# Redistributing rows and columns of one shared piece among the sixteen DMA engines in a grouped 1x1 convolution

## The chip, the cores and the metric

The kernel runs on one core of a Trainium2 chip. The metric is the device time of one execution in microseconds (us), as the median of several runs. The profile is of one execution, and its span goes from the first to the last instruction.

## The reference

The input `x` has shape (1, 512, 512, 192) in bf16 and is read as 262,144 pixels of 192 channels. The kernel size is 1, so there is no neighbourhood and no padding. The channels are split into four groups of 48, and each group is multiplied by a 48 x 48 matrix of its own:

```
H = W = 512;  G = 4;  Cg = 48;  C = 192;  k = 1
xg  = x.reshape(B, H, W, G, Cg)
out = einsum('bhwgc,gcd->bhwgd', xg, w[0, 0])      # reshaped to (B, H, W, C)
```

Every pixel is 384 B in and 384 B out, so 100.66 MB are read and as many written.

## The kernel before

**Ring and pieces.** A ring in SBUF, 128 rows by 520 pixel columns, holds pixels before and after the multiplication; results overwrite inputs in place. It has five slots of 104 columns (`BIG`). `plan_pieces` cuts all pixels into pieces. The first slot is loaded in four pieces of 8, 20, 28 and 32 columns (`HEAD`); then come full pieces of 104 columns by 128 rows; the remainder, smaller than 104 columns, is the last piece. A full piece of n columns gives each of the 128 rows n consecutive pixels, so that a row is one packet of n x 384 B, and each of the 16 DMA engines moves eight rows.

**The shared piece.** After nine full slots one piece is inserted that fills only some rows, by the tuple `SHARED`. Each entry is (first row, rows, parts, columns, queue):

```
SHARED_COLS = 72
SHARED = ((0, 16, 4, SHARED_COLS, SYNC), (32, 16, 4, SHARED_COLS, SYNC), (52, 44, 11, 64, POOL))
CURSOR = 5
```

Two blocks of 16 rows go in four parts through SP's queue (loads) and ACT's queue (stores), so that four DMA engines, called 0 to 3 here, hold eight of these rows each. A block of 44 rows goes in eleven parts through the GpSimd queue; a copy of five rows just before it moves that queue's position, so that engines 5 to 15 hold four of these rows each. Engine 4 holds none of the shared piece. The shared piece holds 32 x 72 + 44 x 64 = 5,120 pixels, and `plan_pieces` gives the other pieces what is left: (262,144 - 5,120) / 128 = 2,008 columns, of which 88 are the head, 18 x 104 the full pieces and 48 the last piece. Rows and columns of the shared piece's slot that hold no pixels are computed too, and not stored.

**Compute.** The unit is a group of four pixel columns. TensorE transposes a group in six 128 x 128 blocks into PSUM (L247), VectorE copies two groups at a time from PSUM to SBUF (L286), TensorE multiplies (L262) with block-diagonal weights that are built at the start, and ScalarE copies the result back into the ring (L304). There are 520 groups, taken in 260 pairs.

**Order.** SP issues the loads (L217) piece by piece. Before the load of a slot it waits until the store of the piece five slots back has landed on all engines (`wait_slot`). ACT issues a store (L298) when the groups of that part have been copied; pieces in the last slots but one are stored in two halves of 52 columns (`LATE_PARTS`), and the last piece, being smaller than 104 columns, in one. GpSimd issues the load and the store of its block (L199), each behind its five-row copy (L197). The DMA engines work the queues of SP, ACT and GpSimd, and instruction fetches, side by side.

Of the kernel before, what the change touches and what calls it, by code (L numbers as in the profile page):

```python
# [28 lines left out]
LATE_PARTS = (52, 52)  # L29
LAST_PARTS = (32, 32, 24, 16)  # L30
SHARED_AT = (9,)
SHARED_COLS = 72
SYNC, POOL = 0, 1
SHARED = ((0, 16, 4, SHARED_COLS, SYNC), (32, 16, 4, SHARED_COLS, SYNC), (52, 44, 11, 64, POOL))
CURSOR = 5
NXP = 4
NXS = 3
# [39 lines left out]
def plan_pieces(npix):  # L77
    few = sum(rows * cols for _, rows, _, cols, _ in SHARED)
    at = list(SHARED_AT)
    if npix < len(at) * few + 128 * (sum(HEAD) + BIG * (at[-1] + 2)):  # L80
        at = []
    cols = (npix - few * len(at)) // 128
    assert cols % 4 == 0
    head = list(HEAD) if cols >= sum(HEAD) + BIG else []
    mid = cols - sum(head)
    slots = [[(BIG, None)]] * (mid // BIG) + ([[(mid % BIG, None)]] if mid % BIG else [])
    for i in at:
        slots.insert(i, [(SHARED_COLS, SHARED)])
    if head:
        slots.insert(0, [(s, None) for s in head])  # L90
    pieces, g, pix = [], 0, 0
    for n, parts in enumerate(slots):
        c = n * BIG % RCOLS
        for s, shares in parts:
            pieces.append(Piece(len(pieces), n, c, g, s, shares, pix))
            c, g, pix = c + s, pieces[-1].g1, pieces[-1].pix_end
    assert pix == npix
    return pieces
# [240 lines left out]
```

## Time and profile before

| | us |
|---|---|
| median of 3 runs | 483.42 (482.58 to 484.23) |
| profiled execution | 483.69 |
| its span | 480.8 |
| PE busy | 430.3 |
| ACT busy | 391.9 |
| DVE busy | 249.6 |
| mean rate of all DMA | 421 GB/s |
| HBM read and written | 100.68 MB and 100.66 MB |

The profile numbers the DMA queues: q1 is SP's, q10 is ACT's, q0 is GpSimd's; q8 and q14 carry instructions. A packet in the trace is one row of one transfer on one engine, with its start, its duration and its size; the record does not name the engine. The semaphore of a transfer rises when an engine has finished its part. PE's busy share counts pipelined matmuls and says little about how near PE is to its peak.

### The profile page before, as it was taken

What the parts mean: (1) busy time and instruction counts of PE and PEld (TensorE: products, weight loads), DVE (VectorE), ACT (ScalarE), POOL (GpSimd) and SP (SyncE); (2) the same over time, 40 slices, a digit from 0 to 9 for tenths busy, and PEclk for the clock granted to TensorE, in tenths of its full rate; (3) what the DMA queues carried; (4) which work ended last, traced back from release to release, by engine and by line L of the source; (5) the groups of instructions that cost most, each with busy time, mean ns of one, the idle gap of its engine ahead of it and who ended that gap; (6) DMA issues with size and microseconds to landing.
All of it is one profiled execution on the core that took longest, in us unless ns stands there. A gap on an engine that the chain in (4) does not pass through costs nothing.

```text
span 480.8 us, 13914 instructions
## 1 busy us (share of the span) xinstructions
PE 430.3 (89%) x6250; PEld 390.5 (81%) x6250; DVE 249.6 (52%) x261; ACT 391.9 (81%) x521; POOL 3.7 (1%) x12
## 2 busy tenths in 40 slices
PE   5979999999999999999679998989898999999910
PEld 5878898898898899889578887978787898898810
DVE  2535655655655655565335553545454556556500
ACT  2959999999998999899649995979797989999920
POOL 1000000000000001000000000000000000000000
PEclk9989999999999999999979998999999999999965
DMA  8999999999999999999999999999999999999995
GB/s 329 428 436 434 413 432 415 413 421 433 428 433 427 438 421 427 423 439 430 428 423 438 434 418 438 435 423 430 431 427 435 432 428 426 420 423 431 428 422 233
DMA packets 7913, 202.22 MB, mean 421 GB/s; under 512 B 1176, under 2 KB 1176, under 8 KB 1688
## 3 DMA queue, kind: packets, MB, share of 16 engines
q1 hardware_dynamic: 3560, 99.60, 48.5%
q10 hardware_dynamic: 4072, 99.58, 48.5%
q0 software_dynamic: 224, 2.16, 1.1%
q8 instruction: 49, 0.80, 0.6%
q14 instruction: 8, 0.07, 0.0%
HBM read 100.68 MB, written 100.66 MB: 419 GB/s over the span
## 4 chain that ended last, share of the span: by engine, by line
PE 47%; another core or an unknown queue 24%; DMA 23%; SPq 1%; issue 1%; ACT 0%
PE o_ps L262 27%; PE xT_ps L247 20%; DMA ring<-in_x_dram 13%; DMA out_dram<-ring 10%; SPq L217 1%; ACT ring L304 0%; SPq L213 0%; SPq L51 0%
## 5 line engine op out<-in xcount | busy, mean ns | idle before, releaser
L304 ACT CAST ring<-o_ps 128x768 bf16<-128x768 f32 x520 | 390.6, 802 | 68.0 <-PE o_ps L262 57.4
L286 DVE COPY xT_sb<-xT_ps 128x1536 bf16<-128x1536 bf16 x260 | 249.0, 958 | 205.1 <-PE xT_ps L247 205.1
L262 PE MATMUL o_ps<-wt,xT_sb 128*128 128x144 bf16 (+1 forms) x3120 | 290.6, 235 | 5.7 <-ACT ring L304 1.8
L262 PEld LDWEIGHTS o_ps<-wt,xT_sb 128*128 128x128 bf16 x3120 | 210.8, 98 | 43.1 <-ACT ring L304 32.8
L247 PE MATMUL xT_ps<-ident,ring 128*128 128x128 bf16 x3120 | 221.6, 222 | 20.9 <-DMA ring<-in_x_dram 20.5
L247 PEld LDWEIGHTS xT_ps<-ident,ring 128*128 128x128 bf16 x3120 | 190.8, 99 | 23.1 <-DMA ring<-in_x_dram 20.1
L197 POOL DMA_DIRECT2D cur<-in_x_dram x2 | 1.2, 622 | 242.7 <-DMA out_dram<-ring 188.8
L230 PE MATMUL o_ps<-w_sb,esel 48*128 48x48 bf16 x10 | 0.6, 209 | 2.8 <-DMA w_sb<-in_w_dram 2.8
L230 PEld LDWEIGHTS o_ps<-w_sb,esel 48*128 48x128 bf16 x10 | 0.4, 111 | 2.8 <-issue 2.8
L280 DVE CAST wt<-o_ps 128x480 bf16<-128x480 f32 x1 | 0.7, 658 | 3.4 <-PE o_ps L230 3.4
L304 ACT ACT_TABLE_LOAD x1 | 1.3, 1283 | 0.8 <-PEq L324 0.8
L199 POOL DMA_DIRECT2D ring<-in_x_dram x1 | 0.6, 563 | 0.0
L199 POOL DMA_DIRECT2D out_dram<-ring x1 | 0.6, 559 | 0.0
L184 POOL TENSOR_SCALAR_AFFINE_SELECT esel<-esel 48x272 bf16<-48x272 bf16 x1 | 0.4, 402 | 0.0
L181 POOL MEMSET esel<- 48x272 bf16 x1 | 0.3, 317 | 0.3 <-POOLq L324 0.3
L188 POOL TENSOR_SCALAR_AFFINE_SELECT ident<-ident 128x128 bf16<-128x128 bf16 x1 | 0.3, 282 | 0.0
L182 POOL MEMSET ident<- 128x128 bf16 x1 | 0.2, 198 | 0.0
L324 POOL MEMSET const-bfloat16-1.0<- 128x1 bf16 x1 | 0.1, 101 | 0.0
L324 POOL MEMSET const-uint8-127<- 128x1 uint8 x1 | 0.1, 101 | 0.0
L324 POOL MEMSET const-float32-0.0<- 128x1 f32 x1 | 0.1, 98 | 0.3 <-issue 0.3
L324 POOL MEMSET const-float32-1.0<- 128x1 f32 x1 | 0.1, 98 | 0.0
## 6 DMA issues: line engine op xcount, KB each, us to landing
ring<-in_x_dram SPq DMA_DIRECT2D x18, 4992.0 KB, 33.4
out_dram<-ring ACTq DMA_DIRECT2D x13, 4992.0 KB, 51.4
out_dram<-ring ACTq DMA_DIRECT2D x10, 2496.0 KB, 43.5
ring<-in_x_dram SPq DMA_DIRECT2D x1, 2304.0 KB, 16.3
out_dram<-ring ACTq DMA_DIRECT2D x1, 2304.0 KB, 19.7
ring<-in_x_dram SPq DMA_DIRECT2D x1, 1536.0 KB, 11.1
out_dram<-ring ACTq DMA_DIRECT2D x1, 1536.0 KB, 40.8
ring<-in_x_dram SPq DMA_DIRECT2D x1, 1344.0 KB, 7.9
```

The costliest lines, as they stand in the source:

```text
L181: gp.memset(esel[:], 1.0).then_inc(p0_sem, 1)
L184: gp.affine_select(out=esel[:], in_=esel[:], pattern=[[-1, ECOLS]], compare_op=AluOpType.is_equal, fill=0.0, base=ESHIFT, channel_multipli ...
L197: gp.dma_start(cur[:, n], few).then_inc(cur_sem, 16)
L199: gp.dma_start(*((sbuf, dram) if inward else (dram, sbuf))).then_inc(done, 16)
L217: sp.dma_start(sbuf, dram).then_inc(ld_sem[p.i], 16)
L230: last = pe.matmul(o_ps[:, NOB - 1, col:col + CG], lhsT=esel[:, s0:s0 + 128], rhs=w_sb[:, g, :], start=True, stop=True, skip_group_check=True)
L247: last = pe.transpose(xT_ps[:, g % NXP, j * 128:(j + 1) * 128], xg[:, j * 128:(j + 1) * 128], ident[:])
L262: last = pe.matmul(o_ps[:, v % NOB, c0_:c1_], lhsT=xs[:, j * 128:(j + 1) * 128], rhs=wt[:, WOFF[tc]:WOFF[tc] + (c1_ - c0_)], start=(tc == ...
L280: dve.tensor_copy(wt[:], o_ps[:, NOB - 1, 0:WCOLS]).then_inc(wc_sem, 1)
L286: dve.tensor_copy(xT_sb[pair % NXS][:, 0:n * 2 * UC].rearrange("p (g c) -> p g c", g=n), xT_ps[:, b0:b0 + n, 0:2 * UC]).then_inc(e_done, 1)
L304: act.copy(dst, o_ps[:, v % NOB:v % NOB + 2, 0:UC]).then_inc(fa_done, 1)
L324: nc = _bacc.Bacc("TRN2", target_bir_lowering=False, num_devices=1)
```

## The change

The two blocks on engines 0 to 3 get 56 columns where they had 72. The block on engines 5 to 15 keeps 64, which is now the widest, so the piece's own size falls from 72 to 64 columns.

```
-SHARED_COLS = 72
+SHARED_COLS = 64
 SYNC, POOL = 0, 1
-SHARED = ((0, 16, 4, SHARED_COLS, SYNC), (32, 16, 4, SHARED_COLS, SYNC), (52, 44, 11, 64, POOL))
+SHARED = ((0, 16, 4, 56, SYNC), (32, 16, 4, 56, SYNC), (52, 44, 11, 64, POOL))
```

By the formula of `plan_pieces` the shared piece now holds 32 x 56 + 44 x 64 = 4,608 pixels, the rest is 2,012 columns, and the last piece has 52 columns instead of 48. The groups become 519: 16 instead of 18 in the shared piece, 13 instead of 12 in the last.

## The prediction

> **What bounds the kernel now.** I read the page first: its busy times, its DMA row, its queue table.
>
> ```profile
> PE 430.3 (89%) x6250; PEld 390.5 (81%) x6250; DVE 249.6 (52%) x261; ACT 391.9 (81%) x521; POOL 3.7 (1%) x12
> ...
> DMA  8999999999999999999999999999999999999995
> ...
> q1 hardware_dynamic: 3560, 99.60, 48.5%
> q10 hardware_dynamic: 4072, 99.58, 48.5%
> q0 software_dynamic: 224, 2.16, 1.1%
> q8 instruction: 49, 0.80, 0.6%
> q14 instruction: 8, 0.07, 0.0%
> ```
>
> No compute engine is over 89%, while the queues add up to 98.7% of sixteen DMA engines' span. The loads are q1, the stores q10, the pool's two copies q0; q8 and q14 fetch instructions through the same engines. The chain of waits names PE (47%), but in a kernel that is full on the DMA side this only says who was late at a buffer. So next the view by windows (columns: stretch, PE, PEld, DVE, ACT, POOL, clock, DMA share, GB/s).
>
> ```profile
> 100.00:190.00 90.00, 89.09 (x1318) 80.58 (x1316) 52.66 (x55) 82.12 (x110) 0.00 (x0) 1.00 1.00 429
> 190.00:300.00 110.00, 99.06 (x1413) 90.20 (x1411) 56.23 (x59) 88.49 (x119) 2.36 (x4) 0.95 1.00 430
> 438.00:468.00 30.00, 20.97 (x306) 18.63 (x304) 12.02 (x13) 21.00 (x28) 0.00 (x0) 0.89 1.00 428
> 468.00:481.00 13.00, 0.00 (x0) 0.00 (x0) 0.00 (x0) 0.00 (x0) 0.00 (x0) 0.50 0.55 238
> ```
>
> After the first 20 us the DMA share stands at 1.00 up to 468, whatever PE does. In the last 13 us no engine computes and the DMA engines finish at different times (share 0.55). The DMA view of the last 3.2 us, in forty slices of 80 ns, and the timeline of ACT's end show the rest:
>
> ```profile
> DMA  0900000000900000005500000000000000000000
> GB/s 0 461 0 0 0 0 0 0 0 0 461 0 0 0 0 0 0 0 230 230 0 0 0 0 0 0 0 0 0 0 0 0 0 0 0 0 0 0 0 0
> DMA packets 8, 0.11 MB, mean 35 GB/s; under 512 B 2, under 2 KB 2, under 8 KB 2
> ```
> ```profile
> 460.67 0.34 ACTq L298 DMA_DIRECT2D out_dram<-ring  x1
> ```
>
> Six large packets, in three pairs: two engines work alone for the last 2.2 us. The last store was issued at 460.67, 19 us earlier, so they are not waiting for anything; they still have a queue. The end is set by whichever DMA engine has most to do.
>
> **Which engine has most.** In the trace's packet records each packet starts 3 ns before the one ahead of it on its engine ends, so sixteen streams can be followed back from their last packets. Their ends, and what the streams hold from 185 us on:
> - three end at 468.1, 468.6, 468.7: pool packets, hardly any fetches;
> - eight end at 475.8, 475.9, 476.1, 476.5, 476.7, 476.7, 476.7, 477.7: most q8 fetches, and pool packets;
> - one ends at 476.2: its packets are longer, 1493 and 1578 ns by turns where others take 1476. It is engine 4 by its sum: without that it would have ended some 7 us ahead of the three;
> - four hold the 27,648 B packets of the blocks of 72 columns, so they are engines 0 to 3: 476.9, 477.3, 480.0, 480.0. The two last also hold the q14 fetches.
>
> Here and there a packet falls to a neighbour in this following; the ends and the 27,648 B packets are clear. The groups check by size: a row of one column costs 768 B in and out, 28.4 ns by the 39,936 B packet (1476 ns for 104 columns one way). Engines 0 to 3 carry 8 x 2008 + 576 = 16,640 of them (472 us), engines 5 to 15 carry 16,320 (463 us), engine 4 16,064 (456 us). The first packets start at 2.3 us. Forty-nine fetches on eight engines make six each and one with seven; at about 1.0 us and 0.3 us for the longer packet behind it, that is the 8 us by which the eight end after the three, and the odd one is the stream at 477.7.
>
> **The change, part by part.**
> 1. *Engines 0 to 3, shared piece.* Each moves 8 packets in and 8 out. A packet falls from 27,648 B (1025 ns) to 21,504 B; on the line between 18,432 B (686 ns) and 39,936 B (1476 ns) that is 799 ns. 16 x 226 ns = 3.62 us less on each.
> 2. *All engines, last piece.* The 512 pixels given up make the last piece 52 columns instead of 48. Each engine moves 8 packets in and 8 out at 742 instead of 686 ns (the 19,968 and 18,432 B packets): 16 x 56 ns = 0.90 us more on each.
> 3. *Compute.* The shared piece falls from 18 groups to 16, the last rises from 12 to 13: 519 groups instead of 520. Twelve matmuls, one ACT copy and half a DVE copy go. One more group now follows the last load: ACT's 802 ns step puts the last store at about 461.5. The earliest stream reaches it at 462.6 + 0.45 (its longer load) = 463.0; a packet started 1.7 us after its issue at the head (1.25 to 2.94), so the three early streams could idle 0.2 us of their 9 us. The rest reach it after 470. Costed at nothing; without that cover it would be 0.8 us.
> 4. *Waits.* SP's load of a slot waits for all sixteen engines of the store five slots back, so the laggards 0 to 3 hold it up (the store issued at 318.4 lands its first twelve parts by 331.7, the last at 346.3, and the load starts at 346.32). Their lag shrinks, so loads start no later. No stall goes away, because the share is 1.00 already. The pool's block, its two cursor copies and the queues they pass stay as they are.
>
> The sum: engines 0 to 3 end 2.72 us earlier (474.1, 474.6, 477.3, 477.3); all others 0.90 later: engine 4 at 477.1, the three at 469.6, the eight at 476.7 to 478.6. What is late next is the stream with the seventh fetch. The end moves from 480.0 to 478.6, 1.4 us earlier: half of what is taken off the old bound, since the new one was 2.3 us behind and is pushed 0.9. The profiled execution, 483.69, has span 480.8 and 2.9 around it; it would become 482.3. It stands 0.27 above the median, 483.42, so the forecast is 482.1.
>
> The size of a fetch is the term without a clean row: its packet is about 1.0 us, what it adds behind it 0.3 to 0.5. Moving one fetch from or to the last of the eight is worth 1.3 us either way, so the gain lies between 0.1 and 2.7; I take the ends as this execution has them.
>
> The Trainium skill ("Runtime: NRT & Kernel Launch", Instruction fetch mechanics) says that instructions come in 16 KiB blocks and that crossing one is mostly hidden; the trace agrees on the block (16,384 B packets), but the eight streams that have them end 8 us after the three that hardly do. By that page alone the full gain of 2.7 us would come.
>
> **Rivals.**
> *Full gain.* If the fetches fall otherwise (one block fewer, as 24 of PE's instructions go, or the odd one on an early stream), the eight end near 477.5, almost level with the pair, and the gain comes up to its own 2.7: 483.42 - 2.7 = 480.7. For it: the odd fetch is a single packet. Against: 24 of PE's 12,500 are 0.2%, a tenth of one of its 49 blocks. 12%.
>
> *One shared ceiling.* If the engines share a limit, balance is worth nothing: the same 201 MB take as long, 483.4. For it: 428 to 430 GB/s in all full stretches. Against: in the last 2.2 us, with fourteen engines silent, the two still take 686 ns for 18,432 B, as when all ran. 8%.
>
> The Trainium skill ("DMA: Bandwidth & Descriptors", Specifications) gives about 358 GB/s of HBM for one core and 27 GiB/s for an engine; by the first the transfer as a whole would bind and this change would do nothing, but the rows show 430 GB/s.
>
> *Slower: engines 0 to 3 don't bind in an ordinary run.* The pair leads by 2.3 us only through q14's eight packets (0.07 MB). Without them it would end near 477.3, the eight would set the end already at 477.7, and the change would add its 0.90: 484.3. It decides once the pair's lead over the eight falls under 0.90 us. A seventh or eighth fetch on the wrong stream (1.3) makes it 485.6. For it: fetch times differ from run to run, and the three runs spread by 1.65 us. Against: the instructions are there in every run, profiled or not, and the profiled run is near the median. 22%.
>
> **How the numbers follow.** The forecast's case gets 58%. A measurement of this kernel tells about 0.3% (1.45 us) from no change, and 1.4 us is right at that line: it splits nearly evenly, 28% faster and 30% same. Full gain adds 12% to faster; the shared ceiling adds 8% to same; the slower case gives 10% to same (its 0.9 us is 0.19%) and 12% to slower. Faster 40%, same 48%, slower 12%. The range goes from 480.6, which takes in the full gain, to 484.2, which takes in all but the far end of the slower case. The forecast's own range is 481.2 to 483.2.
>
> **What would show it.** The packets of the shared piece on q1 and q10 at about 0.80 us; the last large packets in one stream or two near 478.6 and 18 or 19.97 KB large; DMA share still 1.00 up to about 469; in the last stretch a share above 0.55; the last store issued near 461.5; 519 ACT copies. It is wrong if the engines with the small shared packets are again the last, if the share falls below 0.99 in mid-span (a load came late), or if the last streams end after 480.

## The result: 1.3 us less, and the profile after

The changed kernel takes 481.82 us (median of 10 runs, 481.15 to 483.10), the kernel before 483.22 in the same series (median of 10). The ratio is 0.9973, with a 95% interval of 0.9960 to 0.9986: about 1.3 us or 0.27% faster (1.4 us between the medians). The prediction said 482.1 and a gain of 1.4. The profiled execution took 481.49, with a span of 479.4; the span fell by 1.4 us, the rest of its difference (483.69 to 481.49) lies in what surrounds the span, 2.1 us instead of 2.9.

The page after, the same lines:

```profile
PE 429.6 (90%) x6238; PEld 390.7 (81%) x6238; DVE 249.2 (52%) x261; ACT 391.3 (82%) x520; POOL 3.7 (1%) x12
...
DMA  8999999999999999999999999999999999999996
...
q10 hardware_dynamic: 4072, 99.58, 48.6%
q1 hardware_dynamic: 3560, 99.60, 48.6%
...
q8 instruction: 49, 0.80, 0.6%
q14 instruction: 8, 0.07, 0.0%
...
L304 ACT CAST ring<-o_ps 128x768 bf16<-128x768 f32 x519 | 390.0, 802 | 69.6 <-PE o_ps L262 62.7
```

Packets and bytes of every queue are the same to the last digit; only the span over which they are spread is shorter (48.5 to 48.6% each). The windows after (stretch, PE, PEld, DVE, ACT, POOL, clock, DMA share, GB/s):

```profile
100.00:190.00 90.00, 88.99 (x1327) 81.09 (x1325) 52.73 (x56) 82.61 (x111) 0.00 (x0) 1.00 1.00 430
190.00:300.00 110.00, 99.27 (x1439) 90.27 (x1437) 57.30 (x61) 90.05 (x121) 2.37 (x4) 0.97 1.00 430
438.00:468.00 30.00, 22.03 (x320) 19.56 (x318) 12.74 (x14) 21.80 (x29) 0.00 (x0) 0.92 1.00 428
468.00:481.00 13.00, 0.00 (x0) 0.00 (x0) 0.00 (x0) 0.00 (x0) 0.00 (x0) 0.50 0.55 237
```

The stretches in the middle moved as many bytes per us as before; the gain lies in how the last queues end. Three views show that end: the DMA engines from 474.0 to 481.0 us (forty slices of 175 ns; a packet counts in the slice in which it starts, the last one in slice 22), the packet count from 477.8 us on, where before a pair of engines had six large packets left, and the last store on ACT's timeline.

```profile
DMA  7755957575775770075002000000000000000000
```
```profile
DMA packets 4, 0.00 MB, mean 0 GB/s; under 512 B 4, under 2 KB 4, under 8 KB 4
```
```profile
461.68 0.34 ACTq L298 DMA_DIRECT2D out_dram<-ring  x1
```

Nothing that starts after 477.8 is a data packet any more; the last one, begun just before, ends at 478.5. Followed back through the packet records in the same way as before, the sixteen streams end as follows. Where two packets end at the same moment, the following can swap two streams; the set of ends does not depend on that.

| streams | before | forecast | after |
|---|---|---|---|
| engines 0 to 3, without fetches | 476.9, 477.3 | 474.1, 474.6 | 474.3, 474.4 |
| engines 0 to 3, with q14 fetches | 480.0, 480.0 | 477.3, 477.3 | 477.8, 478.0 |
| eight with q8 fetches | 475.8 to 477.7 | 476.7 to 478.6 | 476.7 to 478.5 |
| engine 4 | 476.2 | 477.1 | 477.4 |
| three early | 468.1 to 468.7 | 469.6 | 468.9 to 469.2 |

The bound went from the pair with q14 to one of the eight, as forecast.

### The profile page after: what moved, and what is told of

The parts are those of the page before. It is cut to its first block, busy times and chain, and to the rows that moved or that the text cites. A ratio compares the mean times of both kernels' runs of the same rounds, so it can differ in the third digit from the quotient of the medians.

```text
span 479.4 us, 13889 instructions
## 1 busy us (share of the span) xinstructions
PE 429.6 (90%) x6238; PEld 390.7 (81%) x6238; DVE 249.2 (52%) x261; ACT 391.3 (82%) x520; POOL 3.7 (1%) x12
## 2 busy tenths in 40 slices
DMA packets 7913, 202.22 MB, mean 422 GB/s; under 512 B 1176, under 2 KB 1176, under 8 KB 1688
## 3 DMA queue, kind: packets, MB, share of 16 engines
q10 hardware_dynamic: 4072, 99.58, 48.6%
q1 hardware_dynamic: 3560, 99.60, 48.6%
## 4 chain that ended last, share of the span: by engine, by line
PE 48%; DMA 42%; another core or an unknown queue 5%; issue 1%; ACT 1%; SPq 1%
PE o_ps L262 28%; DMA ring<-in_x_dram 23%; PE xT_ps L247 20%; DMA out_dram<-ring 19%; ACT ring L304 1%; SPq L217 0%; SPq L213 0%
## 5 line engine op out<-in xcount | busy, mean ns | idle before, releaser
L247 PEld LDWEIGHTS xT_ps<-ident,ring 128*128 128x128 bf16 x3114 | 190.3, 99 | 22.2 <-DMA ring<-in_x_dram 19.4
```

The lines of the kernel that those rows point to most:

```text
L247: last = pe.transpose(xT_ps[:, g % NXP, j * 128:(j + 1) * 128], xg[:, j * 128:(j + 1) * 128], ident[:])
```

## The experiments

The theory: all sixteen engines work without a pause, so the time is set by the engine with the largest sum of packets. The rivals: one ceiling shared by all engines, so that balance is worth nothing and the gain came from elsewhere; and, for the terms of the sum, fetches that cost nothing. Ratios are to the kernel before, timed in each run's own series; "above the changed kernel" is the difference of two such ratios.

**One step back the other way.** 88 columns on engines 0 to 3.

Against the kernel before:

```
-SHARED_COLS = 72
+SHARED_COLS = 88
```

> Engines 0 to 3 hold 88 columns of the shared piece, the last piece has 44 columns: the step opposite to the change. Theory (the most loaded DMA engine sets the end): against the kernel before, engines 0 to 3 carry 3.62 us more in the shared piece and 0.90 less in the last, so the last pair of streams ends at 480.0 + 2.7 = 482.7 and the time rises by 2.7 us, ratio 1.0056. Rival (one ceiling shared by all engines; what the change gained came from elsewhere): the bytes are the same, so the ratio is 1.000.

Measured: 485.85 us, ratio 1.0058 (1.0046 to 1.0070), where 1.0056 was expected. The view of the DMA engines from 480.0 to 484.1 (forty slices of 0.1 us) has two streams left, one 0.9 us longer:

```profile
DMA  0300300300300300300300000300000000000000
GB/s 0 165 0 0 165 0 0 165 0 0 165 0 0 165 0 0 165 0 0 165 0 0 0 0 0 165 0 0 0 0 0 0 0 0 0 0 0 0 0 0
```

Their last packets end at 482.4 and 483.3; 482.7 was forecast. The same data took 2.8 us more (0.58% of 483), so a shared ceiling does not set the time.

**One step further.** 40 columns on engines 0 to 3, the last piece 56. This edit and those below are against the changed kernel.

```
-SHARED = ((0, 16, 4, 56, SYNC), (32, 16, 4, 56, SYNC), (52, 44, 11, 64, POOL))
+SHARED = ((0, 16, 4, 40, SYNC), (32, 16, 4, 40, SYNC), (52, 44, 11, 64, POOL))
```

> Engines 0 to 3 hold 40 columns, the last piece has 56: a second step in the direction of the change. Theory: the engines with instruction fetches are the bound now and get 0.90 us more, 478.5 + 0.9 = 479.4, while the streams of engines 0 to 3 end near 471.6 and 475.2. Against the kernel before the time is 0.6 us lower, ratio 0.9988, and it is 0.8 to 0.9 us above the changed kernel. Rival (the blocks on engines 0 to 3 still set the end): another 1.3 us is gained, ratio 0.9946.

Measured: 482.68 us, ratio 0.9994 (0.9985 to 1.0003): it lies 0.0021 above the changed kernel's ratio, 1.0 us, where 0.8 to 0.9 was expected. The last data packet ends at 479.8 (forecast 479.4), alone for its last 1.1 us; the view is from 476.0 to 481.0 (slices of 125 ns):

```profile
DMA  7330933730940830040000030000000000000000
```

So taking still more from engines 0 to 3 loses most of what the first step won: they no longer set the end, and the 0.90 us that everyone gets for it is paid in full. With 88, 72, 56 and 40 columns the ratios are 1.0058, 1, 0.9973 and 0.9994, a V whose two sides are the two terms of the sum.

**The first term alone.** 56 columns, but the last piece stays at 48: this kernel leaves out the last 512 pixels of the image.

```
-    pieces = plan_pieces(npix)
+    pieces = plan_pieces(npix - 512)
```

> The first part of the change alone: engines 0 to 3 hold 56 columns, the last piece keeps 48, and the 512 pixels between (the last of the image) are neither loaded nor computed nor stored. Theory: the pair of engines 0 to 3 ends 3.6 us earlier, at 476.4 to 477.0, the eight with fetches stay at 475.8 to 477.7; the end moves from 480.0 to about 477.7, so 2.3 us less than before, ratio 0.9953, and 0.9 us less than the changed kernel. Rival (shared ceiling): only the 0.2% of bytes left out is gained, 0.9 us, ratio 0.998.

Measured: 480.68 us, ratio 0.9947 (0.9935 to 0.9959), where 0.9953 was expected and the shared ceiling gave 0.998. The last data packet ends at 477.6 (forecast 477.7), the two streams of engines 0 to 3 without fetches at 473.2 and 473.6, 3.7 us earlier than before (forecast 3.6). The bytes left out are 0.39 of 202.22 MB, 0.2%, where the ratio fell by 0.53%:

```profile
DMA packets 7913, 201.83 MB, mean 422 GB/s; under 512 B 1176, under 2 KB 1176, under 8 KB 1688
```

The changed kernel's 0.9973 is 0.0026 above this, 1.3 us for the second term, 0.9 by the sum and between the ends (477.6 and 478.5); the intervals hold both.

**More fetches.** Nothing but instructions is added.

```
+                for _ in range(4):
+                    dve.wait_ge(wb_sem, 1)
```

> The changed kernel with four waits more in each of DVE's 260 steps, on a semaphore that has long been reached: no work and no data, but 1,040 instructions of 64 B, 67 kB or eight fetches of 8,192 B more on q14. Theory (a fetch costs its engine's queue 0.3 us and 0.3 to 0.4 in the packet behind it, and q14 serves one stream of engines 0 to 3 for each engine that fetches): the stream that serves DVE ends 5 to 6 us later, 478 + 5.5 = 483.5, and the time is about 5 us above the changed kernel, ratio to the kernel before 1.007. If they spread over both streams, 2 to 2.5 us above it, ratio 1.002. Rival (crossing a block is hidden, and the end is not set by these streams): the time of the changed kernel, ratio 0.997.

Half as many came out as were meant (why is open); the page counts them (13,889 instructions in the changed kernel):

```profile
span 482.1 us, 14410 instructions
...
q8 instruction: 49, 0.80, 0.6%
q14 instruction: 12, 0.10, 0.0%
```

These are 521 instructions and four fetches more on q14. In the packet records four of q14's twelve stand about where four stood in the changed kernel; the other four have become eight, some 50 to 75 us apart. Measured: 484.61 us, ratio 1.0027 (1.0016 to 1.0039), which is 2.6 us above the changed kernel. The DMA view of the last 3.4 us shows one engine alone:

```profile
DMA  0005000000005000000005000000000000000000
...
DMA packets 4, 0.06 MB, mean 18 GB/s; under 512 B 1, under 2 KB 1, under 8 KB 1
```

It ends at 481.2, the other fifteen by 478.6. The ratio alone would also fit the branch in which eight fetches spread over two streams (1.002); that one stream is late, and that four came instead of eight, is in the trace. Its place before was 477.8 or 478.0, so four fetches cost it 3.2 to 3.4 us, 0.8 us each; the expectation's 0.6 to 0.7 was a little low. So a fetch is not free for the DMA engine that carries it. That one stream took all four also shows that here DVE's fetches went through one DMA engine, on q14, while the 49 blocks on q8 went through several.

**Which engines are early.** The pool's block is split in two, of three and of eight engines; the five-row copy stands before the first alone (that edit is not shown).

```
+SHARED_COLS = 96
+SHARED = ((0, 16, 4, 54, SYNC), (32, 16, 4, 54, SYNC), (52, 12, 3, SHARED_COLS, POOL), (64, 32, 8, 54, POOL))
```

> The pool's block is split: engines 5 to 7 hold 4 rows of 96 columns, engines 8 to 15 4 rows of 54, engines 0 to 3 8 rows of 54; the last piece has 52 columns as in the changed kernel. Theory, with the guess that the three streams that end near 469 are engines 5 to 7: against the changed kernel these three get 3.6 us more (to 472.7), the eight with fetches 1.1 less (477.4), engines 0 to 3 0.45 less (477.6). The end comes near 477.6, ratio to the kernel before 0.995. If the early three are other engines, streams with fetches get the 3.6 us and the end comes near 481 to 482, ratio 1.002 to 1.004. Rival (shared ceiling, or compute: the shared piece has 24 groups, 8 more to compute): no gain over the changed kernel, ratio 0.997 to 1.00.

Measured: 485.00 us (483.49 to 485.47), ratio 1.0030 (1.0019 to 1.0041): the guess that engines 5 to 7 are the early ones was wrong, and the branch for that (1.002 to 1.004) came in. In the profiled execution, 483.80 us, two streams end at 480.9 and 481.2, when all others have ended by 478.1: two of engines 5 to 7 do fetch, one does not.

> A look at which DMA engines the early streams are. The pool's block is cut into five blocks of two engines each, with columns of their own as a mark: engines 5 and 6 hold 50 columns, 7 and 8 54, 9 and 10 58, 11 and 12 62, 13 and 14 64, engine 15 none; the last piece has 56 columns. The size of its shared packets then names a stream's pair. Theory, after the split of 3 and 8 engines: one of engines 5 to 7 and two of 8 to 15 end 7 to 8 us ahead of the others, and hold no 16,384 B fetches, and every stream's end follows its sum. The time itself is no question: by the sums it is 0.5 to 1.5 us above the changed kernel. Rival (the early streams are not tied to engines): the early three show other marks than these groups allow.

The five-row copy stands once before the five loads and, with six rows, once before the five stores. The edit of the tuple (that of the copies is not shown):

```
+SHARED = ((0, 16, 4, 56, SYNC), (32, 16, 4, 56, SYNC),
+          (52, 8, 2, 50, POOL), (60, 8, 2, 54, POOL), (68, 8, 2, 58, POOL), (76, 8, 2, 62, POOL), (84, 8, 2, 64, POOL))
```

One execution was timed: 492.49 us. By the marks, both streams of 54 columns (engines 7 and 8) are without fetches, as is one of the two streams without a mark (engine 15; the other has the longer packets and is engine 4). So engines 7, 8 and 15 are the early ones, and the split before agrees (one of 5 to 7, two of 8 to 15). The time was off by far more than the 0.5 to 1.5 us that was called no question. The reason is in the issues (KB, us from issue to landing) and in the windows:

```profile
ring<-in_x_dram POOLq DMA_DIRECT2D x1, 192.0 KB, 61.5
...
ring<-in_x_dram POOLq DMA_DIRECT2D x1, 186.0 KB, 50.9
...
ring<-in_x_dram POOLq DMA_DIRECT2D x1, 174.0 KB, 38.2
...
ring<-in_x_dram POOLq DMA_DIRECT2D x1, 162.0 KB, 25.4
...
ring<-in_x_dram POOLq DMA_DIRECT2D x1, 150.0 KB, 17.9
```
```profile
190.00:240.00 50.00, 32.75 (x481) 29.33 (x478) 19.32 (x21) 31.14 (x42) 3.39 (x6) 0.88 1.00 429
240.00:300.00 60.00, 42.92 (x619) 39.44 (x619) 24.22 (x26) 37.69 (x50) 3.28 (x6) 0.84 0.98 405
300.00:346.00 46.00, 45.89 (x677) 41.34 (x676) 27.09 (x29) 42.14 (x57) 0.00 (x0) 1.00 0.93 382
```

Five transfers of the pool's queue land one after the other, 8 to 13 us apart, though each has different engines; in the changed kernel a single one of 1,056 KB landed in 19.4 us. The shared piece was complete at 255 us, PE stood for 32 us (its longest wait for a load is 32.3 us), and the queues behind it ran dry: the share falls to 0.98 and 0.93. Compute never caught up; the last store was issued at 478.8 us, 17 us later than in the changed kernel. Here a stall cost time; in the four kernels of the V the share stayed at 1.00 up to 468 us.

**A flatter distribution.** With these marks, engines 7 and 8 were given more and the rest less; the five-row copy stands once before the three transfers (that edit is not shown).

```
-SHARED_COLS = 64
+SHARED_COLS = 104
+SHARED = ((0, 16, 4, 48, SYNC), (32, 16, 4, 48, SYNC),
+          (52, 8, 2, 48, POOL), (60, 8, 2, SHARED_COLS, POOL), (68, 28, 7, 48, POOL))
```

> A try at a flatter distribution, with the marks of the run before: engines 7, 8 and 15 fetch no instructions. Engines 7 and 8 hold 4 rows of 104 columns, engines 5, 6 and 9 to 15 4 rows of 48, engines 0 to 3 8 rows of 48, the last piece has 56 columns; the pool's block goes in three transfers of 2, 2 and 7 engines. By the sums alone, against the changed kernel: the streams with fetches 0.9 us less (477.6), the pair with q14 0.9 less (477.0), engine 4 0.9 more (478.2), engines 7 and 8 5.5 more (474.5): the end near 478, ratio to the kernel before 0.996, about 0.4 us better than the change. Rival (the three pool transfers land one after the other, as the five did in the run before): the shared piece is complete at about 230 us instead of 211, PE stands 5 to 10 us, and if the queues of stores run dry behind it the time is 1 to 5 us above the changed kernel, with a DMA share under 1.00 between 240 and 346 us.

Measured: a median of 487.61 us over twelve runs. Six took 482.3 to 485.6 us, with ratio 1.0007 (0.9991 to 1.0024), so no gain; the other six took 489.6 to 494.2, with granted clocks like the rest (0.957 to 0.974). In the profiled one, 483.59 us, the pool's three loads landed 16.9, 28.2 and 41.0 us after their issue and PE waited up to 12 us for a load, but the share stayed at 1.00, and all streams but two ended by 478.3, as the sums said; two ended at 480.5, and whose they are stays open. Whether the six long runs have the stall of the run before is open too: none of them was profiled. A version that beats the changed kernel was not found.

## Why the prediction was right

- *What bounds.* The prediction read the end as that of the fullest of sixteen engines, from the last two streams working alone for 2.2 us. The V of four column counts and the run with fetches alone show it: each moved the end by about what it put on one group of streams, with the data unchanged. In all of these runs, and with the first term alone, the stream that ends last can be followed back over more than 200 us with no gap above 3 ns between its packets.
- *Engines 0 to 3, 3.62 us less.* The packet of 21,504 B took 799 ns, as the prediction's line between two other sizes gave it. With the first term alone the streams without fetches ended 3.7 us earlier.
- *Last piece, 0.90 more.* The packet took 742 ns. The eight moved from 475.8 to 477.7 up to 476.7 to 478.5.
- *What is late next.* The forecast end of 478.6 was measured at 478.5. The pair with q14 fell only 2.0 to 2.2 us instead of 2.7, to within 0.5 of the new bound; the early three came up to 0.7 sooner than forecast and engine 4 0.3 later. The size of a step was right on the streams that set the end; single streams scatter by half a microsecond, so an agreement within 0.1 us is partly luck. So is the margin: the prediction took the spread of the fetches from one execution and put 1.3 us on one fetch more or less, and the odd block of 49 might have fallen elsewhere.
- *Compute.* The page counts 519 ACT copies. The last store was issued at 461.7 (forecast 461.5) and no stream that sets the end waited for it.
- *Waits.* Loads did start earlier. The store that the prediction reads as held up to 346.3 was complete at 336.6 after, and the load behind it began then, as the chain of work shows (start, us; the first line before, the others after):

```profile
346.32 38.06 DMA ring<-in_x_dram
```
```profile
293.27 43.33 DMA out_dram<-ring
336.62 47.92 DMA ring<-in_x_dram
```

The prediction gives the issue of that store as 318.4; that is the next store, and this one was issued at 294.9 before and 293.3 after. The reading that its last parts hold up the load stands. The 10 us bought nothing that shows: the DMA share was 1.00 around it in both kernels.
- *A sign badly chosen.* A share above 0.55 was expected in the last stretch; it stayed at 0.55. The window is 13 us long in both kernels and holds nearly the same bytes (238 GB/s before, 237 after).
- *The fetch.* Its cost, 1.3 us a block on q8, was the term without a row. The count of 49 stayed, so the change did not depend on it. No run changes it on q8 alone (the pages of 88 columns and of the split in two count 50 blocks); on q14 a fetch of half that size was measured at 0.8.
- *The slower rival*, an end already set by the eight, is out: the first term alone gains 0.53% (2.3 us between the medians), and it could gain nothing if the pair did not lead.
- *The full gain* needed the eight to end near 477.5. They ended at 478.5, and 481.82 us lies 1.1 above that rival's 480.7.
- *The shared ceiling* is out by the V: the data is the same in its four kernels, and their times differ by up to 0.85%.

## What to carry to other kernels

When the DMA share is 1.00 until the queues run out, don't ask first who waits: add up the packets of each DMA engine, its instruction fetches included, and compare the largest sum with the next. Taking work off the fullest engine is worth only the distance to the next one, and what is taken has to go somewhere; here 3.6 us came off four engines and 0.9 went back to all, but the end moved only 1.4, because the next group then set it. A buffer released 10 us earlier was worth nothing that shows while the queues had a backlog. A flatter distribution has a price of its own: with the pool's block in three or five transfers the pieces landed late, and no time was won.

## What the runs showed of the hardware

- Instruction fetches load the DMA engines unevenly here. The 49 blocks of 16,384 B on q8 (PE's by their size: 0.80 MB over its 12,500 instructions and weight loads is about 64 B for each) went over eight engines, 5, 6 and 9 to 14 by the marks. These ended about 8 us after engines 7, 8 and 15, which move the same data. Four more fetches of 8,192 B cost one engine 3.2 to 3.4 us.
- Engine 4 (by its sum) moved most of its 39,936 B packets in about 1.49 us for loads and 1.57 to 1.60 us for stores where the others took 1476 ns, in both kernels; the prediction's 1493 and 1578 are two frequent values. The cause is open.
- Several transfers on the pool's queue beside two full queues landed one after the other: a single one after 19.4 us, the second of two after 26.2, the last of three after 41.0 and the last of five after 61.5, for fewer bytes each. The cause is open.
